# Writing out the order of all engines for the last 108 steps of a fused MLP, with loads of y in two buffers

## The chip, the core and the metric

The kernel runs on one core of one Trainium2 chip. The metric is device time in microseconds from start to end of one execution, as the median of several runs; lower is better. The engines are called as in the profile: PE is TensorE (matmuls; PEld is its weight load), DVE is VectorE, ACT is ScalarE, POOL is GpSimd, SP is SyncE, whose queue issues the DMAs.

## What is computed

Three stages in a row, on 4608 tokens (8 batches of 576) of width 512:

```python
p_packed = sm_attn(p, k, v)                 # 32 packed queries per head
out = sm_attn(q, p_packed, p_packed)        # every query attends to the 32 packed rows
x = out.transpose(0, 2, 1, 3).reshape(4608, 512)
h = np.maximum(x @ w_in, 0.0)               # first MLP, 512 -> 2048 -> 512
y = (h * h) @ w_out
h = y @ w_in2                               # second MLP, 512 -> 1024 -> 512
sm = softmax(h); solu = h * sm
ln = (solu - mean) / sqrt(var + 1e-6) * g_ln
return ln @ w_out2
```

The weights are 64-bit floats; the kernel turns their bits into fp32 on the chip. A product is made of three matmuls of rounded "high" parts and rests ("low" parts): high x high, low x high, high x low.

## The kernel before

**The first MLP** runs as 256 steps (the loop over `t` at the end of `build`; step i is t - 10). A step (b, half, fc) does for one batch b, one half of its 576 tokens (288 columns) and one 128-row slice fc of the 2048 hidden rows:

- `h1`: six matmuls into a PSUM bank (tile `h` in the trace), then ACT takes the ReLU into `rg`, gg = r*r is made on POOL or ACT, gh is the same square rounded (ACT, into `ghl`), and `split_lo` makes the rest gl = gg - gh on DVE (`ghl<-rg,ghl`). The pool gives `rg` two buffers and `ghl` four.
- `ymm`, three steps later (LAG = 3): twelve matmuls of gh and gl with the weights of slice fc, added up in four PSUM tiles `Y`. After 16 slices the four tiles are copied out (`ys<-Y`, two by ACT, two by DVE) and stored to `y_d`; the next step's `ymm` writes the same four tiles.

**Beside them** run jobs that a table (`at_step`) ties to steps:

- `s2_jobs`: the second attention of the next batch (softmax on DVE, POOL and ACT, casts `ah`, rests `al`).
- `load_slot`: loads of the folded first weights (`slot<-pw_d`, 512 KB each).
- `decode_at`, `quads`: the weights of the second MLP are loaded (`raw`), turned into fp32 (`dw`), combined for Strassen's scheme, split into high and low (`op`) and stored (`wi_d`, `wx_d`).
- `pre_y(m)`, for m = 0 to 13 at steps 138 + 6m: a block of 256 tokens of y is read back (`yf<-y_d`), its four quadrants are combined and split into seven operands `yo` (high by an ACT cast, low by POOL or DVE), which are stored (`yc_d<-yo`). `yf` has one buffer, `yo` seven.

**What sets the order.** Matmuls of the first MLP and DMAs are pinned (`pin = tc.keep_in_program_order`), and so are a few ACT copies and all of `operands` in `pre_y`. The rest of ACT, DVE and POOL is placed by a list scheduler at build time. Each engine, and SP's queue, works off its own list strictly in that order.

**The second MLP** follows the 256 steps: 18 blocks of 256 tokens, PE-heavy, its first block `h2(0)` at step 249.

Of the kernel before, what the change touches and what calls it, by code (L numbers as in the profile page):

```python
# [22 lines left out]
P = 128  # L23
# [9 lines left out]
def f(ap):  # L33
    return ap.bitcast(F32)


def build(tc, qT, kT, vP, pT, w_in, w_out, w_in2, w_out2, g_ln, out):
    nc = tc.nc

    TURN = {n: cycle(x) for n, x in {"ETC": "VA", "LNA": "AAAV"}.items()}  # L40
    V, A, G, PE, SP = nc.vector, nc.scalar, nc.gpsimd, nc.tensor, nc.sync


    pin = tc.keep_in_program_order

    def mm(*a, **k):
        pin(PE.matmul(*a, **k))  # L47
# [40 lines left out]

    slc = slc_p.tile([P, 4, 2, 4, 2 * NPK], F32, name="slc")
    G.memset(slc, 0.0)  # L90
    atA, atA_st = pool("atA")
# [15 lines left out]
    class Decode:  # L107
# [10 lines left out]
        def s1(self):  # L118
            pl, n = self.pl, self.shape[0] * self.shape[1]
            w = self.raw.rearrange("p a c w -> p (a c) w")  # L120
            self.lo, self.hi = w[:, :, 0], w[:, :, 1]
            self.w = pl.tile([P, *self.shape], F32, tag="dw", name="dw", bufs=self.bufs[2])
            self.x = self.w.rearrange("p a c -> p (a c)").bitcast(U32)
            pin(A.activation(f(self.x), f(self.hi), AF.Copy, scale=2.0**-112))
            V.tensor_scalar(out=self.x, in0=self.x, scalar1=3, scalar2=None, op0=ALU.logical_shift_left)

        def s2(self):
            x = self.x
# [17 lines left out]
    class Pack:  # L146
# [97 lines left out]
        def pairs(self, k):  # L244
# [6 lines left out]
            for hh in range(2):  # L251
                r = slice(64 * hh, 64 * hh + 64)
                A.activation(slc[r, k, self.bg, :, 32 * hh:32 * hh + 32],
                             tp[r, 2 * P:3 * P].rearrange("p (b c) -> p b c", b=4), AF.Copy, scale=SCALE)
# [6 lines left out]
    ring, clock = [0], [0]  # L261
    later = []

# [67 lines left out]
    def s2_jobs(b, g, qf=None, parts=1):  # L331
# [12 lines left out]
        def j_mm():  # L344
# [3 lines left out]
            for j in range(2):  # L348
                for k in range(2):
                    mm(pb[j][64 * k:64 * k + 64, :HF], slc[:, 2 * g + k, bg, b4, :],  # L350
                       st["qf"][k][:, j * HF:(j + 1) * HF], start=True, stop=True)
            for j in range(2):
                V.transpose(out=st["t"].rearrange("p n j -> p (n j)")[:, j * HF:(j + 1) * HF], in_=pb[j][:, :HF])

        def part(p):
# [30 lines left out]
            def j_fin(c):  # L386
                def go():
# [3 lines left out]
                    A.copy(hi[:, c], st["aT"][:, c])  # L391
                    split_lo(E, lo[:, c], st["aT"][:, c], hi[:, c])
                return go
# [3 lines left out]

        return [j_load, j_mm] + [j for p in range(parts) for j in part(p)]

# [3 lines left out]
    def h1(n):  # L403
# [67 lines left out]
    def decode_at(i, mk):  # L471
        d = {}
        at_step(i, lambda: d.setdefault("u", mk()))
        for j in range(3):
            at_step(i + 4 + (j > 1), lambda: d["u"].step())

# [108 lines left out]
    def quads(dst, n, b11, b12, b21, b22):  # L585
        def sub(out, x, y):
            V.tensor_tensor(out=out, in0=x, in1=y, op=ALU.subtract)

        def split(o, x):
            t = W2["d"].tile([P, 1024], F32R, tag="op", name="op", bufs=5)  # L590
            pin(A.copy(t[:, :n], x))
            V.tensor_tensor(out=t[:, n:2 * n], in0=x, in1=f(t[:, :n]), op=ALU.subtract)
            later.append(lambda: dma(dst[WO.index(o)], f(t[:, :2 * n])))
# [66 lines left out]

    def operands(q, put, eng, keep=lambda x: x):
        a11, a12, a21, a22 = q["11"], q["12"], q["21"], q["22"]

        def comb(out, x, y, op=ALU.subtract):
            e = next(eng)
            return lambda: keep(e.tensor_tensor(out=out, in0=x, in1=y, op=op))

        def split(n, x):
            e = next(eng)

            def go():
                hi, lo, done = put(n)
                keep(A.copy(hi, x))  # L673
                keep(e.tensor_tensor(out=lo, in0=x, in1=f(hi), op=ALU.subtract))  # L674
                done()
            return go

        return [split("11", a11), comb(a21, a21, a22, ALU.add), split("12", a12), comb(a11, a21, a11),
                split("S2", a11), split("S1", a21), comb(a12, a12, a11), split("22", a22), comb(a22, a22, a11),
                split("S3", a22), split("S4", a12)]  # L680

# [3 lines left out]

    R0, RD = 138, 6

    def pre_y(m):
# [3 lines left out]
        def load():  # L692
            t = X["y"].tile([P, 4, 256], F32, tag="yf", name="yf", bufs=1)
            dma(t, y_d[:, :, m * 256:(m + 1) * 256])
            q = quadrants(t[:, :2], t[:, 2:])
            st["ops"] = operands(q, put, cycle([V if x == "V" else G for x in "GGVGGGGVGGG"]), pin)

        def put(n):
# [9 lines left out]
        for k, js in enumerate(((0, 1), (2, 3), (4, 5, 6), (7, 8, 9, 10))):  # L708
            for j in js:
                at_step(i0 + 2 + k, lambda j=j: st["ops"][j]())  # L710

# [4 lines left out]
    for m in range(NPRE):  # L716
        pre_y(m)
    assert R0 + RD * (NPRE - 1) + 10 <= t0

# [18 lines left out]
    def fetch_y(i):  # L738
# [9 lines left out]
        for k in range(2):  # L748
            dma(y2[k], y_d[:, 2 * k:2 * k + 2, m * 256:(m + 1) * 256])
        eng = cycle([V if x == "V" else G for x in "GGGVGGGGVGG"])  # L750
        for j in operands(quadrants(*y2), lambda n: (*ytl[i][n], lambda: None), eng):
            j()

# [108 lines left out]
    for t in range(max(max(j for j in jobs if j != "first"), T0 + N + LAG - 1) + 2):  # L862
# [34 lines left out]
        if t == 9:  # L897
# [8 lines left out]
            for x in early[1]:  # L906
                x.pop(0)()
            early[1] = early[1][0] + early[1][1]
        if 0 <= i < N:
            h1(steps[i])  # L910
        for j in jobs.get(t, ()):
            j()
        products()
        if i == 0:
# [128 lines left out]
```

## Time and profile before

| | us |
|---|---|
| median of 3 runs | 1239.2 (1237.6 to 1242.95) |
| the profiled execution | 1236.75 |
| its span, first to last instruction | 1235.0 |
| PE busy | 1147.7 (93%) |
| DVE / ACT / POOL busy | 858.2 / 665.4 / 585.5 |
| steps 138 to 245 of the first MLP, by their first `h` matmuls | 498.95 to 797.90 |

An engine's idle time counts only where the others wait for it. PE is the engine that is busy nearly throughout, so the reader should look for the places where PE stands, and ask there what it waited for. The shares are averages over stages with different limits; the table's last line bounds the stage that the change touches. The granted clock is a share of 2.4 GHz.

### The profile page before, as it was taken

How to read it: one execution, taken by the hardware profiler on the slowest of the kernel's cores; microseconds unless marked ns; L12 is line 12 of the kernel's file. 1: busy time of each engine (PE TensorE's matmuls, PEld its weight loads, DVE VectorE, ACT ScalarE, POOL GpSimd, SP SyncE). 2: the span in 40 equal slices, each digit the busy share in tenths (PEclk: the TensorE clock that was granted, in tenths of full speed). 3: DMA queues.
4: the chain of work that ended last, by engine and by line, in shares of the span. 5: the costliest groups of instructions: out<-in, count | busy, mean ns of one | idle time of the engine just before them, and what ended most of it. 6: DMA issues, size and time to landing. Idle time of an engine off the chain costs nothing. (4 is left out here: it accounts for less than half of the span.)

```text
span 1235.0 us, 23639 instructions
## 1 busy us (share of the span) xinstructions
PE 1147.7 (93%) x8556; PEld 1057.7 (86%) x8556; DVE 858.2 (69%) x1688; ACT 665.4 (54%) x1493; POOL 585.5 (47%) x606
## 2 busy tenths in 40 slices
PE   6677899999999999989899889999989999999998
PEld 3457799898999998988899889988979889889897
DVE  4868588745327667448658656246989889888886
ACT  3465555444436655455666665334654655655553
POOL 1133255534126544555757655222744654655643
PEclk9788899999999999989999999999999999999999
DMA  9676697665165899489597868974143142223201
GB/s 329 213 215 183 194 289 234 225 219 194 38 228 139 252 293 268 131 305 329 180 351 279 285 244 307 391 274 172 39 134 97 36 149 85 90 96 107 77 23 48
DMA packets 125541, 239.06 MB, mean 194 GB/s; under 512 B 16880, under 2 KB 44528, under 8 KB 125424
## 3 DMA queue, kind: packets, MB, share of 16 engines
q1 hardware_dynamic: 125424, 237.55, 58.1%
q8 instruction: 67, 1.10, 0.3%
q14 instruction: 50, 0.41, 0.1%
HBM read 144.71 MB, written 91.75 MB: 191 GB/s over the span
## 5 line engine op out<-in xcount | busy, mean ns | idle before, releaser
L47 PE MATMUL Y<-ghl,woh 128*128 128x288 f32 x2048 | 470.8, 305 | 20.5 <-ACT ys L445 13.7
L47 PEld LDWEIGHTS Y<-ghl,woh 128*128 128x128 f32 x2048 | 349.7, 192 | 36.9 <-ACT ys L445 15.8
L47 PE MATMUL Y<-ghl,wol 128*128 128x288 f32 x1024 | 306.5, 299 | 0.0
L56 DVE TENSOR_TENSOR ghl<-rg,ghl 128x288 fp32r<-128x288 f32 x256 | 148.4, 584 | 167.4 <-POOL rg L420 107.4
L47 PE MATMUL h<-ah,slot 128*128 128x288 f32 x1024 | 216.9, 301 | 29.1 <-DMA slot<-pw_d 11.1
L420 POOL TENSOR_TENSOR rg<-rg 128x288 f32<-128x288 f32 x190 | 142.6, 751 | 213.8 <-ACT rg L416 199.6
L47 PEld LDWEIGHTS Y<-ghl,wol 128*128 128x128 f32 x1024 | 196.8, 192 | 0.0
L47 PEld LDWEIGHTS h<-ah,slot 128*128 128x128 f32 x1024 | 168.0, 192 | 32.8 <-issue 13.5
L947 POOL TENSOR_TENSOR cl<-raw,ch 128x512 fp32r<-128x512 f32 x100 | 144.5, 1462 | 108.7 <-ACT ch L946 53.6
L768 PE MATMUL o<-wx,ch 128*128 128x256 f32 x1008 | 190.8, 287 | 5.5 <-DVE ys L785 2.8
L416 ACT ACTIVATE rg<-h 128x288 f32<-128x288 f32 x256 | 104.5, 408 | 158.5 <-PE h L47 150.2
L768 PEld LDWEIGHTS o<-wx,ch 128*128 128x128 f32 x1008 | 160.0, 192 | 12.4 <-DVE ys L785 4.3
L47 PE MATMUL h<-al,slot 128*128 128x288 f32 x512 | 152.4, 298 | 0.0
L768 PE MATMUL o<-wx,cl 128*128 128x256 f32 x504 | 142.8, 286 | 1.0 <-DVE cl L947 0.5
L421 ACT ACTIVATE ghl<-rg 128x288 fp32r<-128x288 f32 x256 | 113.2, 442 | 21.7 <-PE Y L47 17.4
L946 ACT CAST ch<-raw 128x512 fp32r<-128x512 f32 x126 | 76.7, 621 | 64.0 <-DVE raw L952 56.0
L768 PEld LDWEIGHTS o<-wx,cl 128*128 128x128 f32 x504 | 95.9, 191 | 3.0 <-POOL cl L947 0.8
L47 PEld LDWEIGHTS h<-al,slot 128*128 128x128 f32 x512 | 97.8, 191 | 0.4 <-POOL al L56 0.4
L674 POOL TENSOR_TENSOR yo<-yf,yo 128x256 fp32r<-128x256 f32 x70 | 60.1, 873 | 65.0 <-ACT yo L673 49.7
L56 POOL TENSOR_TENSOR ws<-dw,ws 128x512 fp32r<-128x512 f32 x32 | 42.5, 1328 | 92.3 <-ACT ws L273 78.8
L768 PE MATMUL h<-wi,y 128*128 128x512 f32 x312 | 83.5, 403 | 0.2 <-DVE hs L785 0.2
L952 DVE TENSOR_TENSOR raw<-raw 128x512 f32<-128x512 f32 x70 | 75.7, 1093 | 7.3 <-ACT raw L962 4.5
(144 smaller groups left out, 1889.8 us busy)
## 6 DMA issues: line engine op xcount, KB each, us to landing
pw_d<-pws SPq DMA_DIRECT2D x124, 256.0 KB, 4.6
slot<-pw_d SPq DMA_DIRECT2D x62, 512.0 KB, 6.1
yc_d<-yo SPq DMA_DIRECT2D x98, 256.0 KB, 5.3
y<-yc_d SPq DMA_DIRECT2D x92, 256.0 KB, 4.5
raw<-w_in SPq DMA_DIRECT2D x40, 512.0 KB, 6.3
raw<-w_out SPq DMA_DIRECT2D x24, 512.0 KB, 6.3
kf<-kT SPq DMA_DIRECT2D x32, 288.0 KB, 5.9
out<-ys SPq DMA_DIRECT2D x72, 128.0 KB, 1.8
```

Of the source, the lines that this page charges most:

```text
L47: pin(PE.matmul(*a, **k))
L56: eng.tensor_tensor(out=lo, in0=x, in1=f(hi), op=ALU.subtract)
L416: A.activation(r, pb[:, :HF], AF.Relu)
L420: G.tensor_tensor(out=gg, in0=r, in1=r, op=ALU.mult)
L421: A.activation(gh, r, AF.Square)
L674: keep(e.tensor_tensor(out=lo, in0=x, in1=f(hi), op=ALU.subtract))
L768: PE.matmul(bk, x, w[:, y], start=(i == 0), stop=(i == 3 * nk - 1))
L946: A.copy(c[n][0], x)
L947: eng.tensor_tensor(out=c[n][1], in0=x, in1=f(c[n][0]), op=ALU.subtract)
L952: eng.tensor_tensor(out=out, in0=x, in1=y, op=op)
```

## The change

For steps 138 to 245 every instruction of ACT, DVE and POOL is pinned to the order in which the program writes it, and the writing is changed:

- `Engine` wraps the three engines and pins while `strict[0]` is set.
- In a strict step the order is: `h1` with its ReLU; rests left over from the last step's `s2_jobs` (`soon`); the step's jobs; the two squares; the rest gl of the *step before* (`lows`); `ymm` and its copies. On odd steps ACT makes gg, on even steps POOL, now up to step 245 (before: up to 229).
- Decoding is spread over steps +4, +5, +6 (before +4, +4, +5), with the shift moved beside its DVE users. `quads` and `operands` make the high parts in one step and the low parts in the next (`low`).
- `pre_y` starts work 4 steps after its load (before 2) over 5 steps; odd blocks load into the memory of `slc`'s first half, now a tile of its own, so that loads alternate between two buffers. Stores go out 2 steps after the low parts.
- The transposes of `s2_jobs` become a job of their own from batch 2 on. In the second MLP, the four blocks made on the spot put other parts of `operands` on DVE (the rests 22 and 12 in place of two combinations).

```diff
+    class Engine:
+        def __getattr__(self, name):
+            fn = getattr(self.e, name)
+            return (lambda *a, **k: pin(fn(*a, **k))) if strict[0] else fn
+    V, A, G = Engine(nc.vector), Engine(nc.scalar), Engine(nc.gpsimd)
...
         A.activation(r, pb[:, :HF], AF.Relu)
-        if clock[0] < T0 + 20 or T0 + R0 <= clock[0] < T0 + t0 and clock[0] % 2:
-            A.activation(gg, r, AF.Square)
-        else:
-            G.tensor_tensor(out=gg, in0=r, in1=r, op=ALU.mult)
-        A.activation(gh, r, AF.Square)
-        split_lo(V, gl, gg, gh)
+        def squares():
+            if t < T0 + 20 or strict[0] and t % 2:
+                A.activation(gg, r, AF.Square)
+            else:
+                G.tensor_tensor(out=gg, in0=r, in1=r, op=ALU.mult)
+            A.activation(gh, r, AF.Square)
+        return squares, lambda: split_lo(V, gl, gg, gh)
...
-        for k, js in enumerate((((split, "11", b11), (sub, b11, b12, b11), (split, "T1", b11)),
-                                ((sub, b12, b22, b12), (split, "22", b22), (sub, b22, b22, b11)),
-                                ((split, "21", b21), (sub, b21, b21, b22), (split, "T3", b12)),
-                                ((split, "T2", b22), (split, "T4", b21)))):
+        for k, js in enumerate(([(split, "11", b11), (split, "21", b21), (split, "22", b22)], [(low,)],
+                                [(sub, b11, b12, b11), (sub, b12, b22, b12), (sub, b22, b22, b11)],
+                                [(split, "T1", b11), (split, "T3", b12)], [(low,), (sub, b21, b21, b22)],
+                                [(split, "T2", b22), (split, "T4", b21)], [(low,)])):
...
+        return [[(split, "11", a11), (split, "12", a12), (split, "22", a22), (comb, a21, a21, a22, ALU.add)], [(low,)],
+                [(split, "S1", a21), (comb, a11, a21, a11), (comb, a12, a12, a11), (comb, a22, a22, a11)],
+                [(low,), (split, "S2", a11), (split, "S4", a12), (split, "S3", a22)], [(low,)]]
...
-            t = X["y"].tile([P, 4, 256], F32, tag="yf", name="yf", bufs=1)
+            if m % 2:
+                t = slc_p.tile([P, 4, 256], F32, tag="sl0", name="yf", bufs=1)
+            else:
+                t = X["y"].tile([P, 4, 256], F32, tag="yf", name="yf", bufs=1)
...
-                k = clock[0] - T0 + 3
+                k = clock[0] - T0 + 2
                 at_step(k, lambda: dma(yc_d[m][:, AO.index(n)], f(t)))
...
+        strict[0] = R0 <= i < 246
+        sq = None
         if 0 <= i < N:
-            h1(steps[i])
+            sq = h1(steps[i])
+        for fn in soons:
+            fn()
+        soons.clear()
+        if sq and not strict[0]:
+            sq[0]()
+            sq[1]()
         for j in jobs.get(t, ()):
             j()
+        if sq and strict[0]:
+            sq[0]()
+        for fn in lows:
+            fn()
+        lows.clear()
+        if sq and strict[0]:
+            lows.append(sq[1])
         products()
```

What this does to ACT's list where the first finished `Y` tiles of the stage are copied out (step 146). Before, with `L673` the casts of `pre_y`, `L445` the copies of `Y`:

```order
L673 CAST yo<-yf 128x256 x2
L416 ACTIVATE rg<-h_6528 128x288
L418 ACTIVATE rg<-rg 128x288
L421 ACTIVATE ghl<-rg 128x288
L416 ACTIVATE rg<-h_6556 128x288
L445 COPY ys<-Y_601 128x288
L421 ACTIVATE ghl<-rg 128x288
L673 CAST yo<-yf 128x256
L445 COPY ys<-Y_603 128x288
L416 ACTIVATE rg<-h_6596 128x288
```

Now (pinned instructions carry the line of the wrapper, L53):

```order
L53 ACTIVATE rg<-h_6517 128x288
L53 CAST yo<-yf 128x256 x3
L53 ACTIVATE rg<-rg 128x288
L53 ACTIVATE ghl<-rg 128x288
L53 ACTIVATE rg<-h_6553 128x288
L53 ACTIVATE ghl<-rg 128x288
L53 COPY ys<-Y_603 128x288
L53 COPY ys<-Y_605 128x288
L53 ACTIVATE rg<-h_6587 128x288
L53 ACTIVATE dw<-raw 128x512
```

The cast that stood between the two copies is gone from there; the copies stand together at the end of their step, behind the step's casts and squares.

DVE's list around step 163, where decoding, `quads` and the copies of `Y` meet. Before:

```order
L56 TENSOR_TENSOR ghl<-rg,ghl 128x288 x2
L592 TENSOR_TENSOR op<-dw,op 128x512
L447 COPY ys<-Y_602 128x288
L592 TENSOR_TENSOR op<-dw,op 128x512
L587 TENSOR_TENSOR dw<-dw 128x512
L447 COPY ys<-Y_604 128x288
L674 TENSOR_TENSOR yo<-yf,yo 128x256
L56 TENSOR_TENSOR ghl<-rg,ghl 128x288
```

Now:

```order
L53 TENSOR_TENSOR ghl<-rg,ghl 128x288 x2
L53 COPY ys<-Y_604 128x288
L53 COPY ys<-Y_606 128x288
L53 TENSOR_SCALAR dw<-dw 128x512
L53 SCALAR_TENSOR_TENSOR dw<-raw,dw 128x512 x2
L53 TENSOR_TENSOR op<-dw,op 128x512 x2
L53 TENSOR_TENSOR dw<-dw 128x512
L53 TENSOR_TENSOR ghl<-rg,ghl 128x288
```

The two copies come at once; behind them a whole decode and three passes of `quads` stand ahead of the next gl.

## Rows read from the trace of the kernel before

**Rows 1.** Windows: stretch us, busy of each engine (count), PEclk, DMA share, GB/s.

```profile
498.95:797.90 298.95, 277.62 (x1978) 270.36 (x1977) 180.05 (x294) 172.93 (x452) 169.38 (x205) 0.97 0.79 280
541.07:560.37 19.30, 19.30 (x146) 19.30 (x145) 7.81 (x14) 10.95 (x29) 9.56 (x13) 1.00 0.97 340
654.99:662.42 7.43, 7.43 (x54) 5.83 (x53) 6.97 (x14) 5.14 (x13) 3.56 (x4) 1.00 1.05 403
...
741.00:745.00 4.00, 4.00 (x18) 4.00 (x18) 0.97 (x1) 1.45 (x4) 2.86 (x4) 0.50 1.07 387
780.00:800.00 20.00, 20.00 (x151) 20.00 (x150) 4.47 (x10) 7.94 (x19) 5.95 (x9) 1.00 1.03 397
```

**Rows 2.** Waits of PE in 498.95:797.90: who, for whom, us in total, times, longest.

```profile
PE Y L47 <- ACT ys L445: 13.2, 5, 4.6
PE h L47 <- DMA slot<-pw_d: 4.0, 1, 4.0
PE Y L47 <- DVE ys L447: 2.1, 3, 1.0
PE Y L47 <- DVE ghl L56: 1.8, 3, 1.1
```

**Rows 3.** Timelines of ACT, PE and SP around 522 to 528: start, us, instruction, idle before.

```profile
527.25 0.40 ACT L673 CAST yo<-yf 128x256 fp32r<-128x256 f32 x1 [3.88 <-DMA yf<-y_d]
527.56 0.39 ACT L445 COPY ys<-Y 128x288 f32<-128x288 f32 x1
...
528.00 0.61 PE L47 MATMUL Y<-ghl,woh 128*128 128x288 f32 x1 [3.80 <-ACT ys L445]
...
522.82 0.57 SPq L53 DMA_DIRECT2D yf<-y_d  x1
```

**Rows 4.** Groups by form on ACT in 498.95:797.90: busy us, mean ns | idle before.

```profile
L421 ACT ACTIVATE ghl<-rg 128x288 fp32r<-128x288 f32 x108 | 47.3, 438 | 1.4
L416 ACT ACTIVATE rg<-h 128x288 f32<-128x288 f32 x108 | 43.8, 405 | 48.6 <-PE h L47 43.7 <-DVE ghl L56 4.6
L673 ACT CAST yo<-yf 128x256 fp32r<-128x256 f32 x98 | 36.5, 401 | 45.1 <-DMA yf<-y_d 21.7 <-POOL yf L666 17.7 <-DMA yc_d<-yo 5.5
...
L124 ACT ACTIVATE dw<-raw 128x512 f32<-128x512 f32 x16 | 10.7, 667 | 7.9 <-DMA raw<-w_out 4.6 <-DMA raw<-w_in 3.3
...
L591 ACT CAST op<-dw 128x512 fp32r<-128x512 f32 x14 | 8.3, 617 | 4.5 <-DVE dw L587 4.5
```

**Rows 5.** The same view for DVE.

```profile
L56 DVE TENSOR_TENSOR ghl<-rg,ghl 128x288 fp32r<-128x288 f32 x110 | 69.8, 639 | 88.5 <-POOL rg L420 56.7 <-ACT ghl L421 29.6 <-ACT yo L673 1.6
...
L129 DVE SCALAR_TENSOR_TENSOR dw<-raw,dw 128x512 uint32<-128x512 uint32 x16 | 14.3, 896 | 0.4
L131 DVE SCALAR_TENSOR_TENSOR dw<-raw,dw 128x512 uint32<-128x512 uint32 x16 | 13.9, 868 | 0.2
L592 DVE TENSOR_TENSOR op<-dw,op 128x512 fp32r<-128x512 f32 x14 | 11.3, 815 | 0.6 <-ACT op L591 0.6
...
L125 DVE TENSOR_SCALAR dw<-dw 128x512 uint32<-128x512 uint32 x16 | 8.8, 552 | 11.0 <-ACT dw L124 10.7
L587 DVE TENSOR_TENSOR dw<-dw 128x512 f32<-128x512 f32 x8 | 6.7, 844 | 0.1
L447 DVE COPY ys<-Y 128x288 f32<-128x288 f32 x14 | 6.3, 449 | 1.8 <-PE Y L47 1.8
```

**Rows 6.** Timelines of DVE and POOL, 514 to 519.

```profile
515.33 0.97 DVE L56 TENSOR_TENSOR ghl<-rg,ghl 128x288 fp32r<-128x288 f32 x1 [0.56 <-POOL rg L420]
...
518.98 0.45 DVE L56 TENSOR_TENSOR ghl<-rg,ghl 128x288 fp32r<-128x288 f32 x1
...
515.25 1.65 POOL L674 TENSOR_TENSOR yo<-yf,yo 128x256 fp32r<-128x256 f32 x2
```

**Rows 7.** Instructions on tile `yc_d` in 498.95:797.90, last line: stores and later loads.

```profile
DMA to landing us min/median/max: 2.0/5.6/9.0
```

**Rows 8.** Waits of PE in the second MLP (834:1235), its longest.

```profile
PE o L768 <- DVE ys L785: 2.8, 3, 1.6
```

More of the change, by code (lines that the diff above doesn't have):

```diff
@@ L87, in build @@
     slc_p, slc_st = pool("slc")
-    slc = slc_p.tile([P, 4, 2, 4, 2 * NPK], F32, name="slc")
-    G.memset(slc, 0.0)
+    slc = [slc_p.tile([P, 4, 4, 2 * NPK], F32, tag=f"sl{bg}", name="slc", bufs=1) for bg in range(2)]
+    for x in slc:
+        G.memset(x, 0.0)
     atA, atA_st = pool("atA")
@@ L124, in s1, with shift @@
             pin(A.activation(f(self.x), f(self.hi), AF.Copy, scale=2.0**-112))
+            if not strict[0]:
+                self.shift()
+        def shift(self):
             V.tensor_scalar(out=self.x, in0=self.x, scalar1=3, scalar2=None, op0=ALU.logical_shift_left)
         def s2(self):
+            if strict[0]:
+                self.shift()
             x = self.x
@@ L261, in build, with soon @@
     ring, clock = [0], [0]
-    later = []
+    later, soons, lows = [], [], []
+    def soon(fn):
+        if strict[0]:
+            soons.append(fn)
+        else:
+            fn()
     class Unit:
@@ L349, in j_mm, with j_tr @@
                 for k in range(2):
[L350 removed]
+                    mm(pb[j][64 * k:64 * k + 64, :HF], slc[bg][:, 2 * g + k, b4, :],
                        st["qf"][k][:, j * HF:(j + 1) * HF], start=True, stop=True)
+            st["pb"] = pb
+            if b < 2:
+                j_tr()
+        def j_tr():
             for j in range(2):
[L353 removed]
+                V.transpose(out=st["t"].rearrange("p n j -> p (n j)")[:, j * HF:(j + 1) * HF], in_=st["pb"][j][:, :HF])
         def part(p):
@@ L396, in part @@
             return [j_max, j_sub, j_exp, j_sum, j_norm, j_back] + fins
-        return [j_load, j_mm] + [j for p in range(parts) for j in part(p)]
+        return [j_load, j_mm] + ([j_tr] if b > 1 else []) + [j for p in range(parts) for j in part(p)]
     gt = {}
@@ L474, in decode_at @@
         for j in range(3):
-            at_step(i + 4 + (j > 1), lambda: d["u"].step())
+            at_step(i + 4 + j, lambda: d["u"].step())
     queue = []
@@ L658, in halves, with operands, low @@
         return [t[:, x * 256:(x + 1) * 256].rearrange("p (a c) -> p a c", a=2) for x in range(2)]
-    def operands(q, put, eng, keep=lambda x: x):
+    def operands(q, put, eng):
         a11, a12, a21, a22 = q["11"], q["12"], q["21"], q["22"]
+        los = []
         def comb(out, x, y, op=ALU.subtract):
-            e = next(eng)
-            return lambda: keep(e.tensor_tensor(out=out, in0=x, in1=y, op=op))
+            eng("c").tensor_tensor(out=out, in0=x, in1=y, op=op)
         def split(n, x):
-            e = next(eng)
+            hi, lo, done = put(n)
+            A.copy(hi, x)
             def go():
-                hi, lo, done = put(n)
-                keep(A.copy(hi, x))
-                keep(e.tensor_tensor(out=lo, in0=x, in1=f(hi), op=ALU.subtract))
+                eng(n).tensor_tensor(out=lo, in0=x, in1=f(hi), op=ALU.subtract)
                 done()
[L676 to L680, printed above, removed]
+            los.append(go)
+        def low():
+            for fn in los:
+                fn()
+            los.clear()
+        return [[(split, "11", a11), (split, "12", a12), (split, "22", a22), (comb, a21, a21, a22, ALU.add)], [(low,)],
+                [(split, "S1", a21), (comb, a11, a21, a11), (comb, a12, a12, a11), (comb, a22, a22, a11)],
+                [(low,), (split, "S2", a11), (split, "S4", a12), (split, "S3", a22)], [(low,)]]
     def quadrants(yl, yr):
@@ L692, in load @@
         def load():
-            t = X["y"].tile([P, 4, 256], F32, tag="yf", name="yf", bufs=1)
+            if m % 2:
+                t = slc_p.tile([P, 4, 256], F32, tag="sl0", name="yf", bufs=1)
+            else:
+                t = X["y"].tile([P, 4, 256], F32, tag="yf", name="yf", bufs=1)
             dma(t, y_d[:, :, m * 256:(m + 1) * 256])
             q = quadrants(t[:, :2], t[:, 2:])
-            st["ops"] = operands(q, put, cycle([V if x == "V" else G for x in "GGVGGGGVGGG"]), pin)
+            st["ops"] = operands(q, put, lambda n: V if n in ("22", "S3") else G)
         def put(n):
@@ L707, in pre_y, with go @@
         at_step(i0, load)
-        for k, js in enumerate(((0, 1), (2, 3), (4, 5, 6), (7, 8, 9, 10))):
-            for j in js:
-                at_step(i0 + 2 + k, lambda j=j: st["ops"][j]())
+        for k in range(5):
+            def go(k=k):
+                for fn, *x in st["ops"][k]:
+                    fn(*x)
+            at_step(i0 + 4 + k, go)
     def open_y():
@@ L749, in fetch_y @@
             dma(y2[k], y_d[:, 2 * k:2 * k + 2, m * 256:(m + 1) * 256])
-        eng = cycle([V if x == "V" else G for x in "GGGVGGGGVGG"])
-        for j in operands(quadrants(*y2), lambda n: (*ytl[i][n], lambda: None), eng):
-            j()
+        for js in operands(quadrants(*y2), lambda n: (*ytl[i][n], lambda: None), lambda n: V if n in ("22", "12") else G):
+            for fn, *x in js:
+                fn(*x)
     NPAIR = NT // 256
```

27 lines of the change are left out of this document (20 added, 7 removed).

## The prediction

> **What bounds the kernel now.** The profiled execution took 1236.75 us with a span of 1235.0, 2.45 under the median of 1239.2; I work out a difference in this execution and take it off the median. I read the windows first, then PE's waits in the window the change touches, then the timelines around the longest of them.
>
> Steps 138 to 245 last 298.95 us [rows 1]. What they would last without a stall follows from an undisturbed piece: 541.07 to 560.37 are eight steps in 19.30 us, 2.41 a step, at granted clock 1.00, with PE busy all the time. Two steps that also carry the 16 matmuls of the second attention take 7.43 [rows 1], 2.6 over two plain ones, and there are two such pairs. So 108 x 2.41 + 5.2 = 265.5, and **33.5 us are lost** in this stage. The waits name 21.1 of them [rows 2]: 15.3 for copies of the finished `Y` tiles (13.2 by ACT, 2.1 by DVE), 4.0 for one late slot load, 1.8 for gl. The other 12.4 carry no wait. They lie behind the long waits: after the 4.0 us wait for the slot, 741 to 745 shows PE busy throughout at clock 0.50 [rows 1], which is the 1.2 GHz level, so those 4 us do 2 us of work; the reader sees there that a wait of 4 us costs 6.
>
> Why the copies come late is seen in one place [rows 3]. PE stands 3.80 us for an ACT copy of `Y` at 527.56. That copy stood in ACT's list behind a cast of `pre_y`, which sat idle for 3.88 us until its load of y landed, and SP issued that load only at 522.82. In total ACT waited 21.7 us for loads of y, 17.7 for POOL's combinations and 5.5 for stores that give `yo` back [rows 4]. So ACT, itself far from full (172.93 of 298.95 us [rows 1]), is blocked by casts whose data is not there, and now and then a copy that PE needs at once stands behind.
>
> **What the change takes away.** The load of y now has 4 steps, 9.6 us, to land before its first cast, and with two buffers it need not wait for the last block's POOL work. Combinations and rests are made a step before their users. The copies follow the squares of their own step with no cast between them. I therefore count all 33.5 us as gone, the clock's part with the waits, and then ask what is late next.
>
> **Copies of Y, next time.** In a strict step the two ACT copies stand last, so all the step's ACT work is ahead of them. The first copy is free when PE needs it if it ends by 2.41 + 0.8 us after the step's start (six `h` matmuls of 0.134 come first; the ReLU waits for them too). The fullest such step is 162: ReLU 0.405, decode 0.667, one `yo` cast 0.401, two `op` casts of 0.617, gh 0.438 and the copy at about 0.4 [rows 3, 4]: 0.8 + 3.55 = 4.35, which is 1.1 late. Step 194 comes by the same count to 0.7, its scaling pass taken at the 0.667 of the other 512-wide pass, with 0.4 carried over; the other five (146, 178, 210, 226, 242) to 0.1 or less. I take 2 us; bounds 0 (ACT ahead of the count) and 6 (a wait of some 2 us in front of two copies).
>
> **The rests gl.** A gl is now queued on DVE behind the jobs of the next step, and DVE may not pass it. Step 163 has two copies, a decode, two rests, a subtraction and gl: 2 x 0.449 + 0.552 + 0.896 + 0.868 + 2 x 0.815 + 0.844 + 0.639 = 6.33 us [rows 5] against 2.41. gl of step n is needed by the third product of `ymm` at step n + 3, 5.9 us after the start of the DVE step that holds it; starting 0.5 late, DVE has room for 5.4. So 0.9 is over at 163, and by the same sums about 2 around step 183 and 2 around 213. Against it: in the order of before, counted likewise, DVE runs nearly 10 us behind the steps around step 199, and all the waits for gl came to 1.8 [rows 2]; the gl there stands earlier in the list, so that is not quite the same. Behind a late gl queue ACT's ReLU two steps on (`rg` has two buffers) and then PE. I take 3, nearer to what the waits of before show; bounds 0 and 6.
>
> These durations hold waits of their own. A gl took 0.45 us at 518.98 but 0.97 at 515.33, while POOL was in two passes on `yo` [rows 6]; two-operand work of DVE and POOL goes one after the other. Over steps 160 to 215 DVE's list sums to 132 us by its mean durations [rows 5] and those of the smaller groups of that view, against 135 of PE time. So DVE has no room in that stretch if its passes meet POOL's more often than now; that is a rival below. The Trainium skill (SBUF — State Buffer, SBUF: two separate sides) has the rule behind it: a VectorE instruction with two SBUF inputs and a GpSimd instruction that reads SBUF exclude each other for the whole instruction, and the one that starts first wins. The rows agree.
>
> **Transfers.** The stage moves its bytes in less time: 298.95 us at 280 GB/s [rows 1] is 83.7 MB, in 265.5 us 315 GB/s. On the mean that is possible, since 780 to 800 moved 397 GB/s at a DMA share of 1.03 [rows 1]. The dense piece is steps 181 to 196: by the order of the changed program SP issues 21 stores of `yo` and 7 of `wx_d` (0.26 MB each), 7 of `wi_d`, 7 slots, 3 `raw` and 2 `yf` (0.52 each), 2 `qf` and one `y_d` (0.59 each), 19.1 MB for 16 steps of 41.2 us with their extra matmuls. At 397 GB/s it takes 48, 7 over; the first 13 of these steps alone issue 16.4 MB, 41 us for 31, so the queue is 10 behind at step 193, and a store from there lands in up to 12 (2.0 is the shortest landing [rows 7]). A `yo` buffer is cast into again 3 steps, 7.2 us, after its store, so for a few steps ACT's casts wait up to 5. ACT can carry some 5 us before PE feels it through gh, but a copy of `Y` (step 194) has no such room. I take 3; bounds 0 and 8, the upper for 350 GB/s (340 at a share of 0.97 [rows 1]): 54.5 us, 13 behind. The Trainium skill (DMA: Bandwidth & Descriptors, Specifications) gives about 358 GB/s as one core's HBM limit, which would put the queue 12 behind and this term at an estimated 7; the row of 397 exceeds that limit, so the row decides.
>
> **The clock** again: single waits of about 1 us showed little slow clock behind them, long ones half their length. With 8 us of waits left I take 2 more; bounds 0 and 4.
>
> **Edits at nothing.** Casts, squares, rests and stores are the same in number; up to step 245 instead of 229 ACT makes gg on odd steps, 8 x 0.44 more on an engine that has 0.85 to 1.3 a step there. PE's order is unchanged until the second MLP. Outside the stage the list scheduler moved some DVE and ACT passes (steps 106 to 135) and matmuls of the second MLP; the longest wait group there is 2.8 in all, 1.6 at most [rows 8], so 0 with bounds of 2 to either side.
>
> **The sum.** 33.5 less 2 + 3 + 3 + 2 = 10 leaves 23.5: the profiled execution 1213.2, the median 1239.2 - 23.5 = **1216**.
>
> **Rivals.**
> (a) *All is hidden.* The slack of three steps takes up every burst, only the clock or the odd us remains: 1239.2 - 33.5 = 1206. For it: DVE was further behind before, at little cost. Against it: step 162's count on ACT.
> (b) *DVE and POOL shut each other out.* Pinned, DVE cannot slip in a pass that POOL does not hinder. If each of the 56 gl of steps 160 to 215 takes 0.97 instead of 0.639 [rows 5, 6], DVE needs 132 + 18.5 = 150.5 us for 135, and PE follows: 15.5 lost there in place of the 3 for gl, some of it long enough for the clock: 1216 + 12.5, about 1228. The sentence above on the SBUF page is the rule that would do it.
> (c) *New waits as large as the old ones.* The copies still come late because ACT stands at casts for data, now for the ring of `yo`: 15.3 of waits with their clock stay, and gl adds its 3 and more; the slot's 6 are won: 1236.
> (d) *Slower, by the DMA queue.* Steps 145 to 226 issue 71.9 MB, counted as above, for 203 us of PE time. If the queue cannot serve this mix faster than the 280 GB/s that the stage had on the mean [rows 1], it needs 257 us: ACT stands at every cast into a `yo` that is still being stored, and PE behind it, 54 us longer, and 1239.2 - 23.5 + 54 = 1270. It makes the kernel slower by more than 0.5% from 296 GB/s downward (71.9 MB in 203 + 33.5 + 6.2 us). Against it: at shares near 1 the rows move 340 to 403 GB/s.
>
> **Chances and range.** Forecast 0.57, (a) 0.12, (b) 0.18, (c) 0.08, (d) 0.05. A difference under 0.5%, 6.2 us, is about what a measurement of this kernel cannot tell from none. Faster is the forecast, (a) and (b): 0.87; the same is (c): 0.08; slower is (d): 0.05. The range: all terms at 0 and the outside 2 better give 1204, a little less likely than (a), so 1205; the upper ends 6 + 6 + 8 + 4 leave 9.5 won, 1230, and 2 for the outside, 1232. It holds (a) and (b) and leaves out (c) and (d).
>
> **What would show it.** In the profile after: steps 138 to 245 in about 275 us; ACT's wait for loads of y near nothing; PE's wait for ACT copies about 2 to 5 us, at steps 162 and 194; waits for gl around steps 163, 183 and 213; a granted clock of 0.99 in the stage. I am wrong if ACT's casts wait for stores of `yo` by tens of us, if DVE's mean gl rises toward 0.97, or if the DMA share stands at 1 with under 330 GB/s.

## The result

The changed kernel takes 1227.3 us (median of 4 runs, 1224.8 to 1228.5) against 1238.4 for the kernel before (4 runs, 1237.5 to 1242.95): a ratio of 0.990 with a 95% interval of 0.9871 to 0.993. The gain is 11 us where 23.5 were forecast.

The windows of the changed kernel (stretch us, busy of each engine with its count, granted clock, DMA share, GB/s) give the stage, its dense part (steps 160 to 215) and three short pieces:

```profile
503.13:790.42 287.29, 274.16 (x1978) 268.32 (x1977) 203.42 (x301) 172.53 (x466) 177.78 (x203) 0.98 0.84 304
556.19:716.65 160.46, 148.19 (x1042) 142.82 (x1041) 133.51 (x197) 100.93 (x276) 111.64 (x125) 0.96 0.86 310
...
627.00:629.40 2.40, 2.37 (x10) 2.38 (x11) 0.39 (x2) 2.33 (x7) 1.85 (x3) 0.50 1.03 416
...
686.34:689.00 2.66, 2.66 (x20) 2.66 (x21) 0.71 (x2) 2.62 (x7) 1.32 (x2) 1.00 0.88 227
...
641.00:645.00 4.00, 4.00 (x32) 4.00 (x31) 1.42 (x4) 1.78 (x6) 1.36 (x2) 1.00 1.05 408
```

Steps 138 to 245 last 287.29 us, 11.7 less than in [rows 1]. Of the 33.5 us lost there before, 21.8 are still lost (287.3 - 265.5). DVE (the third busy time in a row) is busy for 203.4 us instead of 180.05, and in the dense part for 133.5 us. The same steps of the kernel before:

```profile
560.37:717.03 156.66, 145.50 (x1042) 140.12 (x1041) 113.54 (x183) 99.36 (x260) 100.72 (x116) 0.98 0.77 278
```

So 20.0 us came on top there. Part of it is work: 197 passes instead of 183 fall into these steps. The stall-free time of that part is 56 x 2.41 + 5.2 = 140.2 us, so DVE is left 7 us to spare there.

Outside the stage nothing was won: step 138 begins at 503.13 instead of 498.95, and what follows step 245 takes 435.5 us instead of 437.1. In the kernels below, most of them with the same work up to there, step 138 begins anywhere from 499.5 to 505.3, so the start says nothing of the change.

Waits of PE, then of ACT, in the stage (who, for whom, us in total, times, longest):

```profile
PE Y L58 <- DVE ghl L53: 7.2, 4, 2.4
PE Y L58 <- ACT ys L53: 4.6, 3, 2.2
PE Y L58 <- DVE ys L53: 1.3, 2, 1.0
```

```profile
ACT rg L53 <- DVE ghl L53: 51.4, 27, 4.2
ACT yo L53 <- DMA yc_d<-yo: 3.2, 4, 2.2
```

Against [rows 2] and [rows 4]: the 13.2 us for ACT's copies are 4.6, the wait for the slot is gone, and no cast of ACT waits for a load of y (21.7 before; POOL still waits 7.3 us for two of them). In their place stands gl, with 1.8 before and 7.2 now. ACT's ReLU waited 4.6 us for gl before, through the two buffers of `rg`, and waits 51.4 now.

DVE's passes have become longer, as its groups by form show (busy us, mean ns | idle before); [rows 5] had 639, 815 and 844 for the first and the last two:

```profile
L53 DVE TENSOR_TENSOR ghl<-rg,ghl 128x288 fp32r<-128x288 f32 x107 | 75.7, 719 | 51.2 <-ACT ghl L53 26.3 <-POOL rg L53 24.9
L53 DVE SCALAR_TENSOR_TENSOR dw<-raw,dw 128x512 uint32<-128x512 uint32 x32 | 31.4, 980 | 1.1
...
L53 DVE TENSOR_TENSOR op<-dw,op 128x512 fp32r<-128x512 f32 x14 | 12.6, 946 | 0.7 <-ACT op L53 0.7
...
L53 DVE TENSOR_TENSOR dw<-dw 128x512 f32<-128x512 f32 x8 | 7.9, 988 | 0.1
```

**One place read through.** These are lines of the timelines of DVE, ACT and PE around step 185 (start, us, instruction, idle before):

```profile
612.84 2.86 DVE L53 TENSOR_TENSOR op<-dw,op 128x512 fp32r<-128x512 f32 x3
615.63 0.45 DVE L53 TENSOR_TENSOR ghl<-rg,ghl 128x288 fp32r<-128x288 f32 x1
616.00 2.62 DVE L53 TENSOR_TENSOR dw<-dw 128x512 f32<-128x512 f32 x3
618.54 0.99 DVE L53 TENSOR_TENSOR ghl<-rg,ghl 128x288 fp32r<-128x288 f32 x1
619.46 0.96 DVE L53 TENSOR_TENSOR yo<-yf,yo 128x256 fp32r<-128x256 f32 x1
620.34 0.92 DVE L53 TENSOR_TENSOR ghl<-rg,ghl 128x288 fp32r<-128x288 f32 x1
621.18 1.02 DVE L53 TENSOR_SCALAR dw<-dw 128x512 uint32<-128x512 uint32 x1
622.24 1.42 DVE L53 SCALAR_TENSOR_TENSOR dw<-raw,dw 128x512 uint32<-128x512 uint32 x2
623.58 2.43 DVE L53 TENSOR_TENSOR op<-dw,op 128x512 fp32r<-128x512 f32 x2
625.92 0.68 DVE L53 TENSOR_TENSOR dw<-dw 128x512 f32<-128x512 f32 x1
626.53 0.81 DVE L53 TENSOR_TENSOR ghl<-rg,ghl 128x288 fp32r<-128x288 f32 x2
```

```profile
616.16 0.41 ACT L53 ACTIVATE rg<-h 128x288 f32<-128x288 f32 x1 [2.80 <-DVE ghl L53]
...
627.07 0.41 ACT L53 ACTIVATE rg<-h 128x288 f32<-128x288 f32 x1 [3.47 <-DVE ghl L53]
```

```profile
627.03 0.85 PE L58 MATMUL Y<-ghl,woh 128*128 128x288 f32 x2 [2.37 <-DVE ghl L53]
```

None of the DVE lines carries an idle time: DVE has been working without a pause. The gl at 615.63 and 618.54 stand behind three passes on 512 columns each, the two at 626.53 behind six, and PE stops for 2.37 us. Behind that stop the piece 627.0 to 629.4 has a granted clock of 0.50, the 1.2 GHz level. Not every stop of this size has that effect: 686.34 follows a wait of 2.25 us and shows 1.00.

**How long a gl takes.** POOL's timeline beside the same lines of DVE:

```profile
613.98 1.18 POOL L53 TENSOR_TENSOR yo<-yf,yo 128x256 fp32r<-128x256 f32 x1
616.98 1.09 POOL L53 TENSOR_TENSOR al<-aT,ah 128x288 fp32r<-128x288 f32 x1 [1.82 <-ACT ah L53]
...
620.12 0.83 POOL L53 TENSOR_TENSOR rg<-rg 128x288 f32<-128x288 f32 x1
```

The gl at 615.63 starts while POOL stands and takes 0.45 us. The gl at 620.34 starts while POOL is in a pass that ends at 620.95; it takes 0.92 and ends 0.31 after that pass. All gl of the stage are of these two kinds: 56 of 108 start while no POOL pass runs and take 0.44 to 0.46 us; 52 start beside one, end 0.31 to 0.32 us after it and take 1.00 on average. So a gl doesn't run slowly beside POOL, it waits until POOL's pass is over.

**Copies that are late for the same reason.** At step 163 PE waits 2.25 us for a copy by ACT. ACT is late because its ReLU stood 3.87 us for a gl, and that gl was behind three passes of `quads` (lines of the timelines of DVE, ACT and PE):

```profile
560.17 3.51 DVE L53 TENSOR_TENSOR dw<-dw 128x512 f32<-128x512 f32 x3
```

```profile
564.70 0.41 ACT L53 ACTIVATE rg<-h 128x288 f32<-128x288 f32 x1 [3.87 <-DVE ghl L53]
```

```profile
567.67 0.40 PE L58 MATMUL Y<-ghl,woh 128*128 128x288 f32 x1 [2.25 <-ACT ys L53]
```

**One wait that comes from the stores.** At step 193 a cast waits for a store of `yo` while the queue moves 408 GB/s at a share of 1.05 (the window 641 to 645 above). DVE's rest waits behind these casts, a gl stands behind the rest and three passes of `quads`, and PE stops for 1.82 us:

```profile
644.64 0.41 ACT L53 CAST yo<-yf 128x256 fp32r<-128x256 f32 x1 [2.22 <-DMA yc_d<-yo]
```

```profile
646.27 0.57 DVE L53 TENSOR_TENSOR yo<-yf,yo 128x256 fp32r<-128x256 f32 x1 [3.67 <-ACT yo L53]
646.76 2.69 DVE L53 TENSOR_TENSOR dw<-dw 128x256 f32<-128x256 f32 x3
```

```profile
649.88 0.53 PE L58 MATMUL Y<-ghl,woh 128*128 128x288 f32 x2 [1.82 <-DVE ghl L53]
```

### The profile page after: what moved, and what is told of

Read it like the earlier page. It is cut to its first block, busy times and chain, and to the rows that moved or that the text cites. A ratio compares the mean times of both kernels' runs of the same rounds, so it can differ in the third digit from the quotient of the medians.

```text
span 1225.9 us, 23705 instructions
## 1 busy us (share of the span) xinstructions
PE 1146.4 (94%) x8556; PEld 1057.7 (86%) x8556; DVE 876.5 (71%) x1688; ACT 662.4 (54%) x1501; POOL 587.6 (48%) x599
## 5 line engine op out<-in xcount | busy, mean ns | idle before, releaser
L1016 POOL TENSOR_TENSOR cl<-raw,ch 128x512 fp32r<-128x512 f32 x100 | 148.2, 1500 | 96.6 <-ACT ch L1015 51.1
L453 POOL TENSOR_TENSOR rg<-rg 128x288 f32<-128x288 f32 x128 | 93.2, 729 | 182.5 <-ACT rg L446 171.6
L67 DVE TENSOR_TENSOR ghl<-rg,ghl 128x288 fp32r<-128x288 f32 x149 | 80.4, 545 | 87.7 <-POOL rg L453 58.8
L53 DVE TENSOR_TENSOR ghl<-rg,ghl 128x288 fp32r<-128x288 f32 x107 | 75.7, 719 | 51.2 <-ACT ghl L53 26.3
L53 ACT ACTIVATE rg<-h 128x288 f32<-128x288 f32 x108 | 44.1, 408 | 110.5 <-PE h L58 56.2
```

The lines of the kernel that those rows point to most:

```text
L53: return (lambda *a, **k: pin(fn(*a, **k))) if strict[0] else fn
L67: eng.tensor_tensor(out=lo, in0=x, in1=f(hi), op=ALU.subtract)
L1016: eng.tensor_tensor(out=c[n][1], in0=x, in1=f(c[n][0]), op=ALU.subtract)
```

## The experiments

The ratios are to the kernel before, whose median was 1239.5, 1241.5 and 1240.7 in the three sessions that the runs came from. Three theories were to be told apart for the late gl. "Place": it stands behind its step's jobs. "Lock": DVE's and POOL's passes exclude each other, so that DVE's list is too long whatever stands first. "Ring": the two buffers of `rg` carry DVE's delay over to ACT.

### Which part of the change wins

**The loads alone**, in the kernel before: two buffers of `yf`, work 4 steps after the load.

```diff
-            t = X["y"].tile([P, 4, 256], F32, tag="yf", name="yf", bufs=1)
+            if m % 2:
+                t = slc_p.tile([P, 4, 256], F32, tag="sl0", name="yf", bufs=1)
+            else:
+                t = X["y"].tile([P, 4, 256], F32, tag="yf", name="yf", bufs=1)
...
-                at_step(i0 + 2 + k, lambda j=j: st["ops"][j]())
+                at_step(i0 + 4 + k, lambda j=j: st["ops"][j]())
```

> The kernel before with one part of the change alone: loads of y alternate between two buffers and the work on a block starts 4 steps after its load instead of 2. Order as the list scheduler places it. The kernel before took 1238.4. If the loads of y were what made ACT's copies late (21.7 us of ACT's waits, 13.2 of PE's), most of PE's wait for ACT copies goes and with its slow clock some 10 us or more: 1222 to 1230. If the order of ACT and DVE was: 1234 or more, with PE's waits for copies still near 10 us.

Measured: 1219.3 us, ratio 0.9844 (0.9822 to 0.9866). That is better than the whole change. One line each of ACT's and of PE's waits in its stage:

```profile
ACT yo L674 <- DMA yf<-y_d: 0.4, 1, 0.4
```

```profile
PE Y L47 <- ACT ys L446: 4.8, 2, 3.1
```

ACT's wait for loads falls from 21.7 to 0.4 and PE's for its copies from 13.2 to 4.8; the stage takes 283.5 us. What the second buffer and the later start are worth one by one, no run shows.

**The layout without the pinned order.**

```diff
-            return (lambda *a, **k: pin(fn(*a, **k))) if strict[0] else fn
+            return fn
```

> The new layout of the work and the two buffers of y stay, but ACT, DVE and POOL are placed by the list scheduler again in steps 138 to 245 as in the kernel before (pinning off). If the pinned order is what won the 11 us: back to about 1238. If the layout and the earlier loads won them: 1228 or less, with no wait of PE behind a cast that waits for a load of y. If the pinned order costs gain (late gl): below 1224.

Measured: 1219.7 us, ratio 0.9846 (0.9828 to 0.9864), stage 279.8. The gain is there without the pinned order, and it is 7.5 us larger (6.7 by the ratios); the intervals of the two kernels don't meet.

**The pinned order without the loads.**

```diff
-            if m % 2:
-                t = slc_p.tile([P, 4, 256], F32, tag="sl0", name="yf", bufs=1)
-            else:
-                t = X["y"].tile([P, 4, 256], F32, tag="yf", name="yf", bufs=1)
+            t = X["y"].tile([P, 4, 256], F32, tag="yf", name="yf", bufs=1)
...
-            at_step(i0 + 4 + k, go)
+            at_step(i0 + 2 + k, go)
```

> The other part of the change alone: pinned order and layout as in the changed kernel, but loads of y into one buffer and the work on a block 2 steps after its load, as in the kernel before. So far: before 1238.4 to 1239.5, changed kernel 1227, two buffers with the old order 1219.3, new layout with two buffers under the list scheduler 1219.7. If the two buffers earn their 19 us and the pinned order costs some 8 whichever loads it has: 1246 or more, ACT standing at casts that wait for loads of y and everything pinned behind them. If the pinned order makes up for late loads (copies no longer behind casts that wait): 1228 to 1238.

Measured: 1248.6 us, ratio 1.0059 (1.0037 to 1.008), slower than before, as the first expectation had it. Its casts wait for loads again:

```profile
ACT yo L53 <- DMA yf<-y_d: 23.5, 11, 8.1
```

Together the four corners are: old loads 1 under the list scheduler and 1.0059 pinned; new loads 0.985 and 0.990. The loads earn 1.5 to 1.6% under either order, and the pinned order costs 0.5 to 0.6% with either loads. With the old loads the pinned kernel also has the new layout, which with the new loads made no difference (0.9844 and 0.9846).

### What the pinned order loses

**gl ahead of the step's jobs.**

```diff
+        for fn in lows:
+            fn()
+        lows.clear()
         for j in jobs.get(t, ()):
             j()
         if sq and strict[0]:
             sq[0]()
-        for fn in lows:
-            fn()
-        lows.clear()
```

> The rest gl of the step before is written ahead of the step's jobs instead of behind them, for steps 138 to 245; nothing else changes. PE waits 7.2 us for gl in this stage of the changed kernel (1227). Theory 'place' (gl is late because a step's decode, copies and rests are queued ahead of it on DVE): PE's waits for gl fall under 2 us, the slow clock behind them goes too, the stage lasts about 277 us instead of 287, the kernel takes about 1217. Theory 'lock' (DVE and POOL exclude each other, DVE is full in the dense stretch wherever gl stands): DVE is as far behind as before, its jobs are late instead of gl, PE waits as long for copies or ACT for rests: 1224 to 1232.

Measured: 1232.8 us, ratio 0.9955 (0.994 to 0.9969), slower than the changed kernel and just above the range that "lock" gave. PE's waits in its stage:

```profile
PE Y L58 <- ACT ys L53: 5.3, 3, 2.9
PE Y L58 <- DVE ys L53: 3.5, 3, 1.7
PE Y L58 <- DVE ghl L53: 3.3, 2, 1.6
PE h L58 <- DVE t L53: 3.1, 1, 3.1
PE Y L58 <- ACT ghl L53: 2.7, 1, 2.7
```

The wait for gl halves, and what DVE now does later is late in its place: its own copies, and `t` of the second attention. "Place" falls as the cause: 17.9 us of waits stand where 13.1 stood.

**The copies of `Y` ahead of the step's jobs.**

```diff
+        if strict[0] and done[0] < N and done[0] <= i - lag(i) and steps[done[0]][2] == 15:
+            ymm(steps[done[0]])
+            done[0] += 1
         for j in jobs.get(t, ()):
```

> The changed kernel (1227) with the copies of finished Y tiles written ahead of the step's jobs instead of behind them (7 steps); nothing else changes. PE waits 4.6 us for ACT's copies and 1.3 for DVE's in the stage. If these waits come from the step's own ACT work standing ahead, as the prediction counted it: both fall under 1.5 us and with the slow clock behind them the kernel takes 1218 to 1222. If the copies are late because ACT and DVE are already behind when the step begins: waits stay at 4 or more, 1225 to 1229.

Measured: 1230.9 us, ratio 0.9919 (0.9892 to 0.9945), not to be told from the changed kernel. Neither expectation holds: the copies are in time, and nothing is won. Two lines of its waits:

```profile
PE Y L58 <- DVE ghl L53: 10.8, 10, 2.4
...
PE Y L58 <- ACT ys L53: 0.8, 1, 0.8
```

What the copies gain (4.6 to 0.8) the gl loses (7.2 to 10.8). In both runs the order only chooses which result is late.

**54 passes taken from POOL**: ACT makes gg on all steps of the stage.

```diff
-            if t < T0 + 20 or strict[0] and t % 2:
+            if t < T0 + 20 or strict[0]:
```

> The changed kernel (1227) with the square gg made by ACT on all steps of 138 to 245 instead of the odd ones: 54 two-operand passes go from POOL to ACT. Theory 'lock' (DVE's passes are long because POOL's shut them out): DVE's mean gl falls from 0.72 to about 0.65 us, PE's waits for gl fall by half, but ACT has 54 x 0.44 = 24 us more to do: 1220 to 1230, with waits for gl going to waits for ACT copies. Theory 'place': gl's waits of PE stay near 7 us and the copies' waits grow from 4.6: 1228 to 1234.

Measured: 1221.1 us, ratio 0.9865 (0.984 to 0.9889), stage 281.8. The interval of the time meets that of the changed kernel; the passes speak plainly. This is gl in DVE's groups, in the same order on DVE:

```profile
L53 DVE TENSOR_TENSOR ghl<-rg,ghl 128x288 fp32r<-128x288 f32 x107 | 65.0, 618 | 55.4 <-ACT ghl L53 55.4
```

The mean falls from 719 to 618 ns and DVE's busy time in the stage from 203.4 to 186.3 us. PE's waits for gl stay near 7 us (6.7), as "place" had it, and its waits in all are 12.5 us instead of 13.1. What became less is the part without a name: of the 16.3 us lost here (281.8 - 265.5) 3.8 carry no wait, of the changed kernel's 21.8 it is 8.7. Nearly all of this is the clock: 13.6 us of the changed kernel's stage stand at a granted clock of 0.50 and do 6.8 us of work; in this stage it is a quarter of that. Its waits are about as long as before, so this run doesn't show whether shorter passes or chance kept the clock up.

**56 passes of POOL left out** (the combinations of y's quadrants).

```diff
         def comb(out, x, y, op=ALU.subtract):
-            eng("c").tensor_tensor(out=out, in0=x, in1=y, op=op)
+            if not strict[0]:
+                eng("c").tensor_tensor(out=out, in0=x, in1=y, op=op)
```

> The changed kernel (1227) with the combinations of y's quadrants, 56 two-operand passes of POOL in steps 138 to 245, left out of the computation (the operands of the second MLP are then made of the uncombined quadrants); order of all engines otherwise as it is. Theory 'lock': DVE's passes get shorter without any change of DVE's own list: mean gl from 0.72 to 0.62 or less, the 32 decode passes from 0.98 to 0.90, DVE's sum in the stage from 217 to under 200; PE's 7.2 us of waits for gl fall under 3; stage under 280, kernel 1212 to 1220. Theory 'place': DVE's passes stay within 3% of 0.72 and 0.98 or, if they get shorter, PE waits for gl as before: 1224 to 1228.

Measured: 1219.2 us, ratio 0.981 (0.9779 to 0.9841), stage 276.8. gl on DVE, and PE's wait for it:

```profile
L53 DVE TENSOR_TENSOR ghl<-rg,ghl 128x288 fp32r<-128x288 f32 x107 | 63.7, 607 | 53.8 <-ACT ghl L53 32.5 <-POOL rg L53 21.3
```

```profile
PE Y L58 <- DVE ghl L53: 2.1, 3, 1.3
```

DVE's busy time is 180.1 us instead of 203.4 with not one of its instructions changed; the decode passes shorten less than "lock" expected (980 to 940 ns, not 900). POOL's work lengthens DVE's passes, and less of it gives the time back. Only 43 gl start beside a POOL pass with gg on ACT and 32 without the combinations, against 52. By the traces and these two runs the lock is shown. That the longer DVE list is what the pinned kernel pays for is less firm: with gg on ACT the list shrank by 17 us and PE's waits stayed, and only without the combinations do the waits for gl fall with it. The combinations' results also come earlier when nobody makes them, so not all of the 10.5 us of the stage need be the lock's.

**Which engine's order?** DVE alone pinned, and ACT and POOL alone:

```diff
-    V, A, G = Engine(nc.vector), Engine(nc.scalar), Engine(nc.gpsimd)
+    V, A, G = Engine(nc.vector), nc.scalar, nc.gpsimd
```

> Which engine's written order costs the 7.5 us between the list scheduler (1219.7) and the changed kernel (1227)? Here DVE alone keeps its written order in steps 138 to 245; ACT and POOL are placed by the list scheduler. If DVE's own order is the cost (gl behind the step's jobs): 1225 to 1229, PE's waits for gl near 7. If it is what POOL and ACT do against it (passes of POOL started when DVE's run): 1218 to 1222.

```diff
-    V, A, G = Engine(nc.vector), Engine(nc.scalar), Engine(nc.gpsimd)
+    V, A, G = nc.vector, Engine(nc.scalar), Engine(nc.gpsimd)
```

> The opposite of the run beside it: ACT and POOL keep their written order, DVE is placed by the list scheduler. If DVE's own order is the cost: 1218 to 1222, DVE's mean gl near 0.64 as in the list version. If POOL's and ACT's order is: 1225 to 1229, mean gl near 0.72.

Measured: 1232.9 us with DVE pinned (0.9938, 0.9917 to 0.9958) and 1227.8 with ACT and POOL pinned (0.991, 0.9885 to 0.9935). gl in DVE's groups, of the first run and of the second:

```profile
L53 DVE TENSOR_TENSOR ghl<-rg,ghl 128x288 fp32r<-128x288 f32 x107 | 67.2, 640 | 57.3 <-ACT ghl L454 28.5 <-POOL rg L453 27.6 <-PE h L58 1.0
```

```profile
L67 DVE TENSOR_TENSOR ghl<-rg,ghl 128x288 fp32r<-128x288 f32 x109 | 76.0, 703 | 54.6 <-ACT ghl L53 30.8 <-POOL rg L53 21.8 <-POOL rg L453 2.0
```

The long gl come with the written order of ACT and POOL (703 and 719 ns), not with DVE's (640, and 646 with none pinned): 54 and 52 of them start beside a POOL pass in the first two kernels, 44 and 47 in the others. This holds for gl alone; the decode passes take 1003 to 1041 ns with none pinned and 980 in the changed kernel. DVE pinned alone seems to cost in another way: in order, it waits for casts that the scheduler placed elsewhere.

```profile
DVE yo L53 <- ACT yo L714: 26.0, 10, 5.0
```

That line has 14.4 in the changed kernel. That it is what makes PE wait 10.9 us for gl in this run, with short gl, is argued and not shown. So I had expected one culprit and found two costs, and they don't add up: DVE's order alone costs 13 us and ACT's and POOL's 8, both together 7.5.

**A third buffer for `rg`**, at the price of one of the seven `yo`:

```diff
-        rg, g2 = t25("1", "rg"), t25("2", "ghl", F32R)
+        i = clock[0] - T0
+        if R0 < i < t0 - 2 and i % 3 == 0:
+            rg = X["y"].tile([P, KC * P], F32, tag="rg", name="rg", bufs=1)
+        else:
+            rg = t25("1", "rg")
+        g2 = t25("2", "ghl", F32R)
...
-            t = X["y"].tile([P, 512], F32R, tag="yo", name="yo", bufs=7)
+            t = X["y"].tile([P, 512], F32R, tag="yo", name="yo", bufs=6)
```

> The changed kernel (1227) with a third buffer for rg in steps 139 to 227 (every third step; its room is taken from yo, which has six buffers instead of seven). In the changed kernel ACT's ReLU waits 51 us for gl in the stage. Theory 'ring' (DVE's delay reaches PE by the two buffers of rg: ReLU waits for gl, and the copies and squares behind it are late): ACT's wait for gl falls under 25, PE's 13 us of waits under 7, kernel 1217 to 1222. Theory 'lock' (DVE's list is as long as the steps, whatever ACT is allowed to do): waits of PE for gl stay at 6 or more, 1225 to 1230; a wait of casts for stores of yo shows if the sixth buffer is the price.

Measured: 1254.5 us, ratio 1.0106 (1.0071 to 1.0141). Two lines of ACT's waits:

```profile
ACT yo L53 <- DMA yc_d<-yo: 52.3, 12, 8.2
ACT rg L53 <- DVE ghl L53: 5.1, 6, 1.3
```

The ReLU's wait for gl is gone (51.4 to 5.1), so `rg` was indeed what held ACT. But the casts wait 52.3 us for stores, and PE waits 12.3 us for gl, so the run says nothing on what the third buffer would be worth by itself. "Ring" stays open. What the run does show is what a missing seventh `yo` can cost, here beside a third `rg`.

### A faster version than both

**gg on ACT under the list scheduler**, with the new layout, and then with the old layout as well (the kernel before, two buffers, gg on ACT). In the second the edit to the run of the loads alone is:

```diff
-        if clock[0] < T0 + 20 or T0 + R0 <= clock[0] < T0 + t0 and clock[0] % 2:
+        if clock[0] < T0 + 20 or T0 + R0 <= clock[0] < T0 + 246:
```

> New layout and two buffers under the list scheduler (1219.7) with gg made by ACT on all steps of 138 to 245 (which took the pinned kernel from 1227 to 1221). If the lock costs the list order too (its DVE sum in the stage is 202 against 193 before): 1212 to 1217. If the list scheduler already keeps DVE's delays from PE, or ACT's 24 us more come back as late copies: 1218 to 1224.

> The kernel before with two parts only: loads of y in two buffers with the work 4 steps later (1219.3 by itself) and gg made by ACT on all steps of 138 to 245. No pinned order, no new layout. With the new layout under the list scheduler gg on ACT gave 1211.7. If the new layout earns nothing of its own: 1209 to 1214. If its spread decodes and rests are worth something once POOL is relieved: 1215 to 1219.

Measured: 1211.7 us, ratio 0.9757 (0.9734 to 0.978), and 1210.5, ratio 0.9764 (0.974 to 0.9788). Both beat both kernels; the first is just below its lower range, the second within the range for a layout that earns nothing of its own. The dense part of the first, in the windows:

```profile
558.58:701.56 142.98, 141.78 (x1042) 137.18 (x1041) 120.14 (x189) 108.57 (x298) 90.34 (x97) 1.00 0.91 332
```

It takes 143.0 us, 2.8 over the stall-free 140.2, with DVE busy for 120.1 instead of 133.5 (125.0 under the list scheduler with half of gg on POOL); the whole stage takes 271.3 against 265.5 without a stall. By the times gg on ACT is worth 8 to 9 us to either list version and 6 to the pinned one; by the ratios, 10 to 11 and 4.

## Why the prediction came out as it did

- **The forecast of 1216 was missed by 11 us**; the measured time lies in the upper part of the range. A little under half of the gain came.
- **What bounds the kernel, and that the old waits go: right.** ACT's waits for loads of y and PE's for the slot are gone and the stage's loss fell. The run of the loads alone shows that they were the cause named for the late copies, and that this one part is worth 19 to 20 us, most of what the sum gave the whole change. The prediction also gave weight to where the copies stand; in the pinned kernel, moving them ahead won nothing.
- **Copies of `Y`, 2 us: measured 5.9** (4.6 and 1.3), at steps 163, 195 and 211. The first two are the copies of steps 162 and 194 that were named; 211 was put at 0.1 or less. The count of ACT's own work was not what failed: ACT came into these steps late, since its ReLU waited for gl. The upper bound of 6 (a wait of some 2 us in front of two copies) just held it.
- **gl, 3 us: measured 7.2**, with waits of 1.8 to 2.4 at steps 185, 193 and 205 and one of 0.8 at 223. **This is the step that failed.** The 1.8 of step 193 is the stores' as well, so 5.4 are left for gl by itself, inside the bound of 6; but the late copies come from late gl too. The sums of DVE used the durations of before, and the waits of before (1.8) pulled the value down. But the passes themselves became longer. gl went from 639 to 719 ns, and by the pinned order: without it the mean is 645 and 646. Two of the 512-wide ones went from 815 to 946 and from 844 to 988, and there the new loads alone, in the old order, bring 910 and 920.
- **Stores, 3 us: measured 1.8** directly, at step 193, where the sum had the queue furthest behind; it moved 408 GB/s, near the 397 that the sum took. It is the wait counted under gl above, and three passes of `quads` stood in that chain too. The upper bound has a slip: its 13 us behind, at 350 GB/s, are those of the end of the piece; at step 193, where the 10 were taken, it would be 16.4 MB in 46.9 us against 31.3, 15.5 behind.
- **The clock, 2 us: measured 6.8**, the term furthest off, above its bound of 4. It was sized for single waits of 1 us. Here they were of about 2, and behind four of the five places with them (163, 185, 193, 211) the granted clock stood at 0.50, 13.6 us in all; behind 205 it stayed at 1.00. The part of the loss without a wait is 8.7 (21.8 less 13.1); 1.9 of it has no cause named here.
- **Outside, 0 with 2 to either side: measured 2.6 worse** in the profiled execution, 4.2 at the start, where the code is the same to step 105, and 1.6 better at the end. That is over the bound of 2; the start lies within what the other runs show.
- **Rival (b)** gave 1228 and had the mechanism. That its time came out is luck in part. Its 135 us leave out the 5.2 of the second attention's matmuls, which fall into these steps; with 140.2 the rival gives about 1223. gl went to 719 ns and not to 970, but every other two-operand pass of DVE grew with it, more passes fell into these steps, and DVE's busy time there rose by 20.0 us where the rival had 18.5. The Trainium skill (SBUF — State Buffer, SBUF: two separate sides) states the exclusion; the trace agrees, with the 52 gl that end just after POOL's passes, and so do the runs with fewer passes on POOL, with 618 and 607 ns for gl against 719. It deserved more than 0.18: the row of a gl that took 0.97 beside POOL [rows 6] and the count of 132 us of DVE work for 135 stood in the same paragraph, and they were not put together in the sum.
- **Rivals (a), (c), (d)**: the slack hides bursts only under the list scheduler with less on POOL (271.3 us); casts don't wait for stores by tens of us unless the ring is cut to six; the queue moved 304 GB/s in the stage and over 400 where it was full, so it did not bound it.

What stays open: why POOL's and ACT's written order makes gl meet POOL's passes more often than the scheduler's does, how much of the 7.5 us the lock is and how much DVE's own order, and what a third `rg` would give with seven `yo`.

## What to carry to other kernels

Try the parts of a change one by one: here the loads in two buffers were worth more than the whole, and the order written out by hand took 7.5 us back. Where an engine's list nearly fills its stage, moving an urgent result forward may only choose another one to be late, as it did in both runs here; take work away from it, or from the engine that shuts it out. Before adding up an engine's durations for a fuller stage, look for the same instruction in a quiet and in a crowded place and calculate with both.

## What the runs showed of the hardware that I had not expected

- A subtraction of DVE that starts beside a pass of POOL ends 0.31 to 0.32 us after that pass, in all 52 cases of the stage, and takes 1.00 us on average instead of 0.45.
- Moving 54 two-operand passes from POOL to ACT shortened 107 gl on DVE from 719 to 618 ns on average, in the same order, and is worth 6 to 9 us to the kernel by the times (4 to 11 by the ratios), although POOL was busy for only 62% of the stage.
- One output buffer of seven can decide: with six (and a third `rg`), casts waited 52.3 us for stores instead of 3.2, and the stage went from 287.3 to 312.6 us, with the DMA share falling to 0.79.
- Behind two waits of PE of almost the same length (2.37 and 2.25 us) the granted clock was 0.50 and 1.00.
